# Sliding-window attention and a SoLU feed-forward layer on one core: lower weight halves by TensorE, a new order at the start, and a lag of one tile

## The chip, the core and the metric

The kernel runs on one core of one Trainium2 chip. A core has five engines that run their own instruction queues in order and meet at semaphores: TensorE (PE; its weight loads are PEld), VectorE (DVE), ScalarE (ACT), GpSimd (POOL) and SyncE (SP), which here only issues DMAs. The metric is the device time of one execution in microseconds (us). The median of three runs of the kernel before is 604.31 us (603.89 to 605.40).

## The reference

Eight batches of 576 tokens, eight heads of 64 columns, give 4608 rows of 512 columns. Attention looks back over a window of 64 tokens, and its output goes through a feed-forward layer with an inner width of 1024:

```python
scores = scale * np.matmul(q, k.transpose(0, 1, 3, 2))
mask = (rel >= 0) & (rel < window)
...
attn = np.exp(scores)
attn = attn / (np.sum(attn, axis=-1, keepdims=True) + 1e-09)
x = np.matmul(attn, v)            # regrouped to 4608 x 512
h = x @ w_in                      # 512 -> 1024
sm = np.exp(h - h_max) / (sum + 1e-09)
solu = h * sm
ln = (solu - mu) / np.sqrt(var + 1e-06) * g_ln
return ln @ w_out                 # 1024 -> 512
```

q, k, v are float32. w_in and w_out come as 64-bit floats.

## The kernel before

**Tiles.** The 4608 rows are 36 tiles of 128 rows. For each tile t the kernel runs:

- `load(t)`: DMAs of q, k and v.
- `scores(t)`: 32 small matmuls into the PSUM tile pS.
- `softmax(t)`: on DVE eight mask-and-minimum operations (L353), on ACT eight exponentials (L358), on DVE the sums' reciprocals (L366, L369), on POOL eight scalings (L371).
- `transposes(t)`: on PE (L387) in two groups of four into the PSUM tile t, copied by ACT and by DVE to PT (L392).
- `values(t)`: 32 matmuls into pX (L411), copied by ACT as the upper half xH (L417) and by DVE as the lower half xL (L418).
- `moe_in(t, h)`: 12 matmuls for each half h of the 1024 columns, into pH (L434).
- `moe_norm(t)`: DVE maximum (L449), ACT exponential (L451), DVE product and sum (L454), ACT squares (L460), a few 128x1 steps, a power on POOL (L467), and on POOL the scaled result e in two halves (L471).
- `moe_transpose(t)`: PE (L491), ACT cast to yH (L495), DVE yL (L497).
- `moe_out(t)`: 24 matmuls into pO (L508), a copy (L515) and the output's DMA (L516).

Products of the feed-forward layer are made as upper x upper, upper x lower and lower x upper, with the halves in a faster float32 form of TensorE (fp32r). pS, pH, pX and pO have one buffer each, so `moe_in(t+1, 0)` waits until `moe_norm(t)` has read pH for the last time, in L454.

**Weights.** `weight_block` turns one 128x512 block of a 64-bit weight into its two halves: a DMA of the raw words (L255), ACT's absolute value of the upper word (L256), DVE's clamp (L257), three integer steps on DVE (L259, L261, L263), for w_out a multiplication by g on POOL (L266), ACT's cast to the upper half (L268), and POOL's subtraction that gives the lower half (L269). Blocks 0 to 7 are w_in (0 to 3 the first half of the columns), 8 to 15 are w_out. The raw words have 4 buffers, the work tile wt has 3. This runs once, at the start.

**Order.** The body only records operations in a `Plan`: engine, estimated cost, tiles read and written. `Plan.edges` turns tiles, buffer rings and program order into dependencies; operations on PE also keep the program's order among each other, and the first uses of a ring's tiles begin in the program's order. `Plan.order` gives each operation a due time, walked back from PE's sequence, and then, engine by engine, takes the ready operation that is due first. The outcome is each engine's fixed queue; the costs have no other effect. The main loop puts `moe_in`, `moe_norm` and the attention of later tiles in iteration t, and `moe_transpose` and `moe_out` of tile t - BEHIND, with BEHIND = 3. So `moe_in` of tiles 0 to 3 runs before the first `moe_out`.

Of the kernel before, what the change touches and what calls it, by code (L numbers as in the profile page):

```python
# [9 lines left out]
F32 = mybir.dt.float32  # L10
# [13 lines left out]
NEG = -8.0e9  # L24

AHEAD = 3
BEHIND = 3

URGENT = 300

# [9 lines left out]
class Plan:  # L40
# [8 lines left out]
        self.tiles = {}  # L49
        self.ops = []  # L50

    def op(self, engine, cost, emit, reads, writes, lat=0):
        self.ops.append((engine, cost, emit, reads, writes, lat + self.LATENCY))

    def dma(self, size, emit, reads, writes):
        self.op("SP", max(350, size // 250), emit, reads, writes, 2000)

    def edges(self):

        before = [dict() for _ in self.ops]  # L60
        writer, readers, users, pe = {}, {}, {}, None
        for i, (engine, _, _, reads, writes, _) in enumerate(self.ops):
            for key in reads + writes:
                if key in writer:
                    before[i][writer[key]] = True
            for key in writes:
                for j in readers.pop(key, ()):
                    before[i][j] = True
                writer[key] = i
            for key in reads:  # L70
                readers.setdefault(key, []).append(i)
            for key in reads + writes:
                if key[0] in self.rings:
                    users.setdefault(key[:2], []).append(i)
            if engine == "PE":
                if pe is not None:
                    before[i].setdefault(pe, False)
                pe = i
        for (tag, n), at in users.items():
            instances = [m for g, m in users if g == tag]  # L80
            place = instances.index(n)
            if place >= self.rings[tag]:
                for j in users[tag, instances[place - self.rings[tag]]]:
                    for i in at:
                        if j != i:
                            before[i][j] = True
            if place:

                j = users[tag, instances[place - 1]][0]
                if j != at[0]:  # L90
                    before[at[0]].setdefault(j, False)
        for i, b in enumerate(before):
            b.pop(i, None)
        return before

    def order(self):
# [16 lines left out]
        for i, o in enumerate(self.ops):  # L113
            if o[0] == "PE":
                due[i] = clock
                clock += o[1]
        for j in reversed(topo):
            for i, whole in after[j]:
                lat = self.ops[j][5] if self.ops[i][0] != self.ops[j][0] else 0
                due[j] = min(due[j], due[i] - (self.ops[j][1] + lat if whole else 0))  # L120
        left = [len(b) for b in before]
        ready = [0] * n
        free = dict.fromkeys(("PE", "DVE", "ACT", "POOL", "SP"), 0)
# [27 lines left out]
def tile_window_attention_solu_moe(  # L151
# [80 lines left out]
    def weight_block(i, src, wH, wL, g, key):  # L234


        n = wH.shape[-1]

        def raw():
            return T("raw", i, [P, n, 2], I32)  # L240

        def t():
            return T("wt", i, [P, n], I32)

        def tf():
            return t().bitcast(F32)

        def lo():
            return raw()[:, :, 0]

        def hi():
            return raw()[:, :, 1]

        R, W = ("raw", i), ("wt", i)
        plan.dma(P * n * 8, lambda: nc.sync.dma_start(raw().rearrange("p n w -> p (n w)"), src), [], [R])  # L255
        plan.op("ACT", 600, lambda: nc.scalar.activation(tf(), hi().bitcast(F32), AF.Abs), [R], [W])  # L256
        plan.op("DVE", 420, lambda: nc.vector.tensor_scalar(  # L257
            tf(), tf(), EXP_LO, EXP_HI, ALU.max, ALU.min), [W], [W])
        plan.op("DVE", 420, lambda: nc.vector.tensor_scalar(  # L259
            t(), t(), 0x07FFFFFF, 3, ALU.bitwise_and, ALU.logical_shift_left), [W], [W])  # L260
        plan.op("DVE", 680, lambda: nc.vector.scalar_tensor_tensor(  # L261
            t(), hi(), -0x40000000, t(), ALU.bitwise_and, ALU.bitwise_or), [R, W], [W])
        plan.op("DVE", 680, lambda: nc.vector.scalar_tensor_tensor(  # L263
            t(), lo(), 29, t(), ALU.logical_shift_right, ALU.bitwise_or), [R, W], [W])
        if g is not None:
            plan.op("POOL", 700, lambda: nc.gpsimd.tensor_scalar(  # L266
                tf(), tf(), g, 0.0, ALU.mult, ALU.add), [W, ("g",)], [W])
        plan.op("ACT", 600, lambda: nc.scalar.copy(wH, tf()), [W], [("H", *key)])  # L268
        plan.op("POOL", 1300, lambda: nc.gpsimd.tensor_sub(wL, tf(), wH.bitcast(F32)),  # L269
                [W, ("H", *key)], [("L", *key)])  # L270

    def prep(i):
        if i < 2 * NC:
# [19 lines left out]
    def V(t, half):  # L293
        return T(f"v{half}", t, [P, DM])

    def load(t):
        first = first_of(t)
        o = t * P

        plan.dma(P * P * 16, lambda: nc.sync.dma_start(  # L300
            Q(t), qT[:, :, o:o + P].rearrange("p d s -> d p s")), [], [("q", t)])
        lack = 0 if t else WIN
        plan.dma(P * P * 24, lambda: nc.sync.dma_start(
            K(t)[:, :, lack:], kT[:, :, o - WIN + lack:o + P].rearrange("p d s -> d p s")),
            [], [("k", t)])
# [19 lines left out]
    def scores(t):  # L325
# [15 lines left out]
                            PS(t)[half * WIN:(half + 1) * WIN, r, p],  # L341
                            q[rs, p, half * WIN:(half + 1) * WIN], keys, start=True, stop=True)

        plan.op("PE", 1000, emit, [("q", t), ("k", t)], [("pS", t)])

    def softmax(t):
        def cols(tag, h):
# [15 lines left out]
        def rec():  # L363
            return T("rec", t, [P, H], pool=st)
# [2 lines left out]
            rec(), T("sm", t, [P, H], pool=st), 1e-9),  # L367
            [("sm", t, h) for h in range(H)], [("rec", t)])
        plan.op("DVE", 130, lambda: nc.vector.reciprocal(rec(), rec()), [], [("rec", t)])  # L369
        for h in range(H):  # L370
            plan.op("POOL", 360, lambda h=h: nc.gpsimd.tensor_scalar(  # L371
                SS(t)[:, h], SS(t)[:, h], rec()[:, h:h + 1], 0.0, ALU.mult, ALU.add),
                [("rec", t)], [("sS", t, h)])

# [3 lines left out]
    def transposes(t):  # L378
        for x in range(2):
# [6 lines left out]
                for i in range(4):  # L386
                    nc.tensor.transpose(pA()[:, i], SS(t)[:, 4 * x + i], ident)  # L387

            plan.op("PE", 430, emit, [("sS", t, 4 * x + i) for i in range(4)], [("t", n)])
            plan.op(  # L390
                "DVE" if x else "ACT", 600, lambda x=x, pA=pA:
                (nc.vector.tensor_copy if x else nc.scalar.copy)(PT(t)[:, 4 * x:4 * x + 4], pA()),  # L392
# [11 lines left out]
    def values(t):  # L404
        def emit():
            for p in range(NPAIR):
# [6 lines left out]
                            PT(t)[:, h, ks], start=True, stop=True)  # L413

        plan.op("PE", 1100, emit, [("PT", t, x) for x in range(2)]
                + [(f"v{half}", t, x) for half in range(2) for x in range(2)], [("pX", t)])
        plan.op("ACT", 560, lambda: nc.scalar.copy(XH(t), PX(t)), [("pX", t)], [("xH", t)])  # L417
        plan.op("DVE", 620, lambda: nc.vector.tensor_sub(XL(t), PX(t), XH(t).bitcast(F32)),  # L418
                [("pX", t), ("xH", t)], [("xL", t)])
# [3 lines left out]
    def PH(t):  # L423
        return T("pH", t, [P, DFF], pool=ps_h)
# [3 lines left out]

    def moe_in(t, h):
        hs = slice(h * 512, (h + 1) * 512)  # L430
        for c in range(NC):
            for k, (x, w, keys) in enumerate((
                    (XH, w_inH, ["xH", "H"]), (XH, w_inL, ["xH", "L"]), (XL, w_inH, ["xL", "H"]))):
                plan.op("PE", 233, lambda c=c, k=k, x=x, w=w: nc.tensor.matmul(  # L434
                    PH(t)[:, hs], x(t)[:, c], w[:, c, hs],
                    start=(c == k == 0), stop=(c == NC - 1 and k == 2)),
                    [(keys[0], t), (keys[1], "in", c, h)], [("pH", t)])

    def moe_norm(t):
        def col(x):  # L440
# [79 lines left out]
            f(t, *args)  # L520


    load(0)
    for i in range(4):
        prep(i)
    scores(0)
    softmax(0)
    load(1)
    for i in range(4, 8):
        prep(i)  # L530
# [1 line left out]
    scores(1)  # L532
    softmax(1)
    values(0)
    load(2)
    scores(2)
    softmax(2)
    plan.dma(P * NF * 4, lambda: nc.sync.dma_start(g_sb, gT), [], [("g",)])
    for i in range(8, 16):
        prep(i)  # L540
    load(3)
    for t in range(NTILE + BEHIND):
        on(load, t + AHEAD + 1)
        on(moe_in, t, 0)
        on(transposes, t + 1)
        on(moe_in, t, 1)
        on(moe_norm, t)
        on(moe_transpose, t - BEHIND)
        on(values, t + 1)
        on(scores, t + AHEAD)  # L550
        on(softmax, t + AHEAD)
        on(moe_out, t - BEHIND)
# [39 lines left out]
```

## Time and profile before

| what | us |
|---|---|
| median of the runs | 604.31 |
| profiled execution, whole | 604.69 |
| its span, first to last instruction | 602.5 |
| PE busy | 563.9 |
| DVE busy | 322.0 |
| ACT busy | 313.3 |
| POOL busy | 210.2 |

The profiled execution lies 0.38 us above the median, and 2.19 us of it are outside the span. The 50.73 MB read from memory contain 8.4 MB of raw weights. A profile line of a group names the kernel line, the engine, the operation, output <- input with shapes, the count, then busy time and mean ns, then the idle time of the engine just ahead of these instructions and what ended it. A line of the timeline begins with the start and the duration in us. A line of the windows gives the window, its length, and the busy time of PE, PEld, DVE, ACT and POOL with the number of instructions, then the granted clock of TensorE, the DMA share and GB/s.

### The profile page before, as it was taken

What the parts mean: (1) busy time and instruction counts of PE and PEld (TensorE: products, weight loads), DVE (VectorE), ACT (ScalarE), POOL (GpSimd) and SP (SyncE); (2) the same over time, 40 slices, a digit from 0 to 9 for tenths busy, and PEclk for the clock granted to TensorE, in tenths of its full rate; (3) what the DMA queues carried; (4) which work ended last, traced back from release to release, by engine and by line L of the source; (5) the groups of instructions that cost most, each with busy time, mean ns of one, the idle gap of its engine ahead of it and who ended that gap; (6) DMA issues with size and microseconds to landing.
All of it is one profiled execution on the core that took longest, in us unless ns stands there. A gap on an engine that the chain in (4) does not pass through costs nothing.

```text
span 602.5 us, 12551 instructions
## 1 busy us (share of the span) xinstructions
PE 563.9 (94%) x4608; PEld 459.3 (76%) x4608; DVE 322.0 (53%) x1180; ACT 313.3 (52%) x933; POOL 210.2 (35%) x438
## 2 busy tenths in 40 slices
PE   1387699999999999999999999999999999999997
PEld 1256578888888888888888888888888888888775
DVE  6768997555555555555555555555555555554430
ACT  3467666555555555555555555555555555553421
POOL 4554668333333333333333333333333333331110
PEclk9988889999999999999999999999999999999999
DMA  8882753333333333333333333333333331000000
GB/s 296 254 262 93 204 157 95 92 91 97 93 95 98 95 97 97 94 93 96 89 98 97 96 97 97 97 97 97 97 97 97 97 97 54 18 18 18 18 36 35
DMA packets 56204, 60.97 MB, mean 101 GB/s; under 512 B 3408, under 2 KB 40272, under 8 KB 56144
## 3 DMA queue, kind: packets, MB, share of 16 engines
q1 hardware_dynamic: 56144, 60.18, 32.7%
q8 instruction: 36, 0.59, 0.4%
q14 instruction: 24, 0.20, 0.1%
HBM read 50.73 MB, written 9.44 MB: 100 GB/s over the span
## 4 chain that ended last, share of the span: by engine, by line
PE 90%; DVE 5%; ACT 2%; POOL 1%; DMA 1%; issue 1%; SPq 0%; ACTq 0%
PE pO L508 35%; PE pH L434 34%; PE pX L411 6%; PE t L387 6%; PE pS L340 5%; PE t L491 5%; DVE wt L261 1%; DMA raw<-w_in 1%; DVE wt L263 1%; DVE sS L353 1%; DVE e L454 1%; POOL sS L371 1%; ACT sS L358 1%; POOL w_inL L269 0%; DVE wt L259 0%
## 5 line engine op out<-in xcount | busy, mean ns | idle before, releaser
L371 POOL TENSOR_SCALAR sS<-sS,rec 128x128 f32<-128x128 f32 x288 | 105.0, 386 | 258.6 <-PE pO L508 257.1
L358 ACT ACTIVATE sS<-sS,nmx 128x128 f32<-128x128 f32 x288 | 112.3, 391 | 52.9 <-DVE nmx L353 52.9
L434 PE MATMUL pH<-w_inH,xH 128*128 128x512 f32 x288 | 119.2, 414 | 8.6 <-DVE mst L454 8.6
L508 PE MATMUL pO<-w_outH,yH 128*128 128x512 f32 x288 | 117.7, 409 | 1.2 <-ACT yH L495 1.2
L434 PE MATMUL pH<-w_inH,xL 128*128 128x512 f32 x288 | 116.3, 404 | 0.0
L434 PE MATMUL pH<-w_inL,xH 128*128 128x512 f32 x288 | 116.0, 403 | 0.0
L508 PE MATMUL pO<-w_outH,yL 128*128 128x512 f32 x288 | 114.3, 397 | 0.0
L508 PE MATMUL pO<-w_outL,yH 128*128 128x512 f32 x288 | 113.9, 395 | 0.0
L495 ACT CAST yH<-t 128x512 fp32r<-128x512 f32 x72 | 38.7, 589 | 101.6 <-PE t L491 101.6
L449 DVE TENSOR_REDUCE mst<-pH 128x1 f32<-128x1024 f32 x36 | 44.1, 1224 | 70.5 <-PE pH L434 70.5
L392 DVE COPY PT<-t 128x512 f32<-128x512 f32 x36 | 24.9, 691 | 89.5 <-PE t L387 89.5
L434 PEld LDWEIGHTS pH<-w_inH,xH 128*128 128x128 f32 x288 | 55.3, 192 | 21.0 <-DVE mst L454 5.8
L471 POOL TENSOR_SCALAR e<-e,mst 128x512 f32<-128x512 f32 x72 | 54.9, 769 | 41.3 <-DVE mst L468 39.9
L508 PEld LDWEIGHTS pO<-w_outH,yH 128*128 128x128 f32 x288 | 54.1, 188 | 18.5 <-ACT e L451 4.8
L434 PEld LDWEIGHTS pH<-w_inH,xL 128*128 128x128 f32 x288 | 55.4, 192 | 13.5 <-DVE xL L418 0.2
L508 PEld LDWEIGHTS pO<-w_outH,yL 128*128 128x128 f32 x288 | 54.1, 188 | 14.6 <-DVE yL L497 1.7
L434 PEld LDWEIGHTS pH<-w_inL,xH 128*128 128x128 f32 x288 | 55.5, 193 | 11.7
L508 PEld LDWEIGHTS pO<-w_outL,yH 128*128 128x128 f32 x288 | 54.2, 188 | 11.6 <-POOL w_outL L269 0.2
L392 ACT COPY PT<-t 128x512 f32<-128x512 f32 x36 | 21.1, 585 | 76.5 <-PE t L387 76.5
L353 DVE CUSTOM_DVE_ANT_0 sS<-pS,maskNone 128x128 f32<-128x128 f32 x224 | 51.3, 286 | 14.0 <-PE pS L340 14.0
L387 PE MATMUL t<-ident,sS 128*128 128x128 f32 x288 | 42.0, 283 | 12.9 <-POOL sS L371 12.7
L358 ACT ACTIVATION_READ_ACCUMULATOR sS<-sS,nmx 128x1 f32 x288 | 53.9, 187 | 0.0
(54 smaller groups left out, 722.1 us busy)
## 6 DMA issues: line engine op xcount, KB each, us to landing
v<-vS SPq DMA_DIRECT2D x64, 256.0 KB, 4.1
k<-kT SPq DMA_DIRECT2D x35, 384.0 KB, 4.0
q<-qT SPq DMA_DIRECT2D x36, 256.0 KB, 4.6
y<-ot SPq DMA_DIRECT2D x36, 256.0 KB, 2.0
raw<-w_in SPq DMA_DIRECT2D x8, 512.0 KB, 5.2
raw<-w_out SPq DMA_DIRECT2D x8, 512.0 KB, 5.2
v<-vS SPq DMA_DIRECT2D x16, 128.0 KB, 4.5
k<-kT SPq DMA_DIRECT2D x1, 256.0 KB, 7.8
```

The lines of the kernel that those rows point to most:

```text
L340: nc.tensor.matmul(PS(t)[half * WIN:(half + 1) * WIN, r, p], q[rs, p, half * WIN:(half + 1) * WIN], keys, start=True, stop=True)
L353: plan.op("DVE", 215, lambda h=h: nc.vector.tensor_tensor_reduce(SS(t)[:, h], PS(t)[:, h % 2, h // 2], mk, scale=-SCALE, scalar=BIG, op0=A ...
L358: plan.op("ACT", 390, lambda h=h: nc.scalar.activation(SS(t)[:, h], SS(t)[:, h], AF.Exp, bias=cols("nmx", h), scale=-1.0, accum_out=cols(" ...
L371: plan.op("POOL", 360, lambda h=h: nc.gpsimd.tensor_scalar(SS(t)[:, h], SS(t)[:, h], rec()[:, h:h + 1], 0.0, ALU.mult, ALU.add), [("rec", ...
L387: nc.tensor.transpose(pA()[:, i], SS(t)[:, 4 * x + i], ident)
L392: (nc.vector.tensor_copy if x else nc.scalar.copy)(PT(t)[:, 4 * x:4 * x + 4], pA()),
L411: nc.tensor.matmul(PX(t)[r * D:(r + 1) * D, p, ks], V(t, half)[:, h * D:(h + 1) * D], PT(t)[:, h, ks], start=True, stop=True)
L434: plan.op("PE", 233, lambda c=c, k=k, x=x, w=w: nc.tensor.matmul(PH(t)[:, hs], x(t)[:, c], w[:, c, hs], start=(c == k == 0), stop=(c == NC ...
L449: plan.op("DVE", 1150, lambda: nc.vector.tensor_reduce(nmax(), PH(t), axis=AX.X, op=ALU.max, negate=True), [("pH", t)], [key(0)])
L471: plan.op("POOL", 770, lambda h=h, hs=hs: nc.gpsimd.tensor_scalar(E(t)[:, hs], E(t)[:, hs], nmean(), kk(), ALU.add, ALU.mult), [key(4), ke ...
L495: plan.op("ACT", 560, lambda hs=hs, pT=pT: nc.scalar.copy(YH(t)[:, hs], pT()), [("t", n)], [("yH", t, h)])
L508: plan.op("PE", 233, lambda f=f, k=k, y=y, w=w: nc.tensor.matmul(PO(), y(t)[:, f], w[:, f], start=(f == k == 0), stop=(f == NF - 1 and k = ...
```

## The change

- Lower halves. For blocks 0 to 7 (`LOWER`) two matmuls into a PSUM tile of the ring t, identity x w (float32) and minus identity x upper half (fp32r), and an ACT copy out. For blocks 8 to 15 a DVE subtraction. POOL makes none.
- The clamp L257 goes to POOL except in blocks 0 and 1 (`QUICK`).
- The scalings of tile 0's softmax go from POOL to DVE.
- PE operations marked loose (the lower halves; `scores`, `transposes`, `values` of tiles 0 to 2) lose their fixed place in PE's order and are placed by due time. SP's DMAs now keep the program's order.
- Program order: q and k of tile 0 first, block 0, scores and softmax of tile 0, block 1, v of tile 0, blocks 2 and 3; `load(2)` between blocks 11 and 12; scores and softmax of tile 2 inside the first iteration.
- `moe_in(0, h)` sorts its passes so that those with lower weight halves come last.
- BEHIND = 1: tile t - 1 instead of t - 3 is transposed and multiplied by w_out in iteration t. The ring e falls from 4 buffers to 2.
- Estimated costs of weight steps and DMAs are changed (340 for 420, 610 for 680, 340 bytes per ns for 250).

```diff
-BEHIND = 3
+HASTE = 1
+QUICK = (0, 1)
+LOWER = range(8)
+LOOSE = 3
+BEHIND = 1
...
-            if engine == "PE":
-                if pe is not None:
-                    before[i].setdefault(pe, False)
-                pe = i
+            if engine in last and not loose:
+                if last[engine] is not None:
+                    before[i].setdefault(last[engine], False)
+                last[engine] = i
...
-                clock += o[1]
+                clock += 0 if o[6] else o[1]
...
+    minus = const.tile([P, P], F32R, name="minus")
+    nc.vector.tensor_scalar_mul(minus, ident, -1.0)
...
-        plan.op("DVE", 420, lambda: nc.vector.tensor_scalar(
+        engine, e, cost = ("DVE", nc.vector, 340) if i in QUICK else ("POOL", nc.gpsimd, 750)
+        plan.op(engine, cost, lambda: e.tensor_scalar(
             tf(), tf(), EXP_LO, EXP_HI, ALU.max, ALU.min), [W], [W])
...
-        plan.op("POOL", 1300, lambda: nc.gpsimd.tensor_sub(wL, tf(), wH.bitcast(F32)),
-                [W, ("H", *key)], [("L", *key)])
+        if i not in LOWER:
+            plan.op("DVE", 610, lambda: nc.vector.tensor_sub(wL, tf(), wH.bitcast(F32)),
+                    [W, ("H", *key)], [("L", *key)])
+            return
+        def pL():
+            return T("t", f"w{i}", [P, n], pool=ps_t)
+        def emit():
+            nc.tensor.matmul(pL(), ident, tf(), start=True, stop=False)
+            nc.tensor.matmul(pL(), minus, wH, start=False, stop=True)
+        plan.op("PE", 1150, emit, [W, ("H", *key)], [("t", f"w{i}")], loose=True)
+        plan.op("ACT", 560, lambda: nc.scalar.copy(wL, pL()), [("t", f"w{i}")], [("L", *key)])
...
+        engine, v, cost = ("POOL", nc.gpsimd, 360) if t else ("DVE", nc.vector, 150)
         for h in range(H):
-            plan.op("POOL", 360, lambda h=h: nc.gpsimd.tensor_scalar(
+            plan.op(engine, cost, lambda h=h: v.tensor_scalar(
...
+        passes = [(c, *k) for c in range(NC) for k in (
+            (XH, w_inH, "xH", "H"), (XH, w_inL, "xH", "L"), (XL, w_inH, "xL", "H"))]
+        if t == 0:
+            passes.sort(key=lambda k: k[4] == "L")
...
-    load(0)
-    for i in range(4):
-        prep(i)
+    load(0, range(2))
+    prep(0)
     scores(0)
     softmax(0)
+    prep(1)
+    load(0, range(2, 4))
+    for i in range(2, 4):
+        prep(i)
     load(1)
     for i in range(4, 8):
         prep(i)
...
     values(0)
-    load(2)
-    scores(2)
-    softmax(2)
     plan.dma(P * NF * 4, lambda: nc.sync.dma_start(g_sb, gT), [], [("g",)])
-    for i in range(8, 16):
+    for i in range(8, 12):
+        prep(i)
+    load(2)
+    for i in range(12, 16):
         prep(i)
     load(3)
     for t in range(NTILE + BEHIND):
         on(load, t + AHEAD + 1)
         on(moe_in, t, 0)
+        if t == 0:
+            scores(2)
+            softmax(2)
+        if t < BEHIND:
+            on(moe_in, t, 1)
+            on(moe_norm, t)
+            on(transposes, t + 1)
+            on(scores, t + AHEAD)
+            on(softmax, t + AHEAD)
+            on(values, t + 1)
+        else:
             on(transposes, t + 1)
             on(moe_in, t, 1)
             on(moe_norm, t)
             on(moe_transpose, t - BEHIND)
             on(values, t + 1)
             on(scores, t + AHEAD)
             on(softmax, t + AHEAD)
             on(moe_out, t - BEHIND)
```

More of the change, by code (lines that the diff above doesn't have):

```diff
@@ L50, in __init__, with op @@
         self.ops = []
-    def op(self, engine, cost, emit, reads, writes, lat=0):
-        self.ops.append((engine, cost, emit, reads, writes, lat + self.LATENCY))
+    def op(self, engine, cost, emit, reads, writes, lat=0, loose=False):
+        self.ops.append((engine, cost, emit, reads, writes, lat + self.LATENCY, loose))
     def dma(self, size, emit, reads, writes):
-        self.op("SP", max(350, size // 250), emit, reads, writes, 2000)
+        self.op("SP", max(350, size // 340), emit, reads, writes, 2000)
     def edges(self):
         before = [dict() for _ in self.ops]
-        writer, readers, users, pe = {}, {}, {}, None
-        for i, (engine, _, _, reads, writes, _) in enumerate(self.ops):
+        writer, readers, users, last = {}, {}, {}, {"PE": None, "SP": None}
+        for i, (engine, _, _, reads, writes, _, loose) in enumerate(self.ops):
             for key in reads + writes:
@@ L119, in order @@
                 lat = self.ops[j][5] if self.ops[i][0] != self.ops[j][0] else 0
-                due[j] = min(due[j], due[i] - (self.ops[j][1] + lat if whole else 0))
+                due[j] = min(due[j], due[i] - (HASTE * (self.ops[j][1] + lat) if whole else 0))
         left = [len(b) for b in before]
@@ L256, in weight_block @@
         plan.op("ACT", 600, lambda: nc.scalar.activation(tf(), hi().bitcast(F32), AF.Abs), [R], [W])
-        plan.op("DVE", 420, lambda: nc.vector.tensor_scalar(
+        engine, e, cost = ("DVE", nc.vector, 340) if i in QUICK else ("POOL", nc.gpsimd, 750)
+        plan.op(engine, cost, lambda: e.tensor_scalar(
             tf(), tf(), EXP_LO, EXP_HI, ALU.max, ALU.min), [W], [W])
-        plan.op("DVE", 420, lambda: nc.vector.tensor_scalar(
+        plan.op("DVE", 340, lambda: nc.vector.tensor_scalar(
             t(), t(), 0x07FFFFFF, 3, ALU.bitwise_and, ALU.logical_shift_left), [W], [W])
-        plan.op("DVE", 680, lambda: nc.vector.scalar_tensor_tensor(
+        plan.op("DVE", 610, lambda: nc.vector.scalar_tensor_tensor(
             t(), hi(), -0x40000000, t(), ALU.bitwise_and, ALU.bitwise_or), [R, W], [W])
-        plan.op("DVE", 680, lambda: nc.vector.scalar_tensor_tensor(
+        plan.op("DVE", 610, lambda: nc.vector.scalar_tensor_tensor(
             t(), lo(), 29, t(), ALU.logical_shift_right, ALU.bitwise_or), [R, W], [W])
@@ L294, in V, with load @@
         return T(f"v{half}", t, [P, DM])
-    def load(t):
+    def load(t, parts=range(4)):
         first = first_of(t)
         o = t * P
-        plan.dma(P * P * 16, lambda: nc.sync.dma_start(
-            Q(t), qT[:, :, o:o + P].rearrange("p d s -> d p s")), [], [("q", t)])
         lack = 0 if t else WIN
-        plan.dma(P * P * 24, lambda: nc.sync.dma_start(
-            K(t)[:, :, lack:], kT[:, :, o - WIN + lack:o + P].rearrange("p d s -> d p s")),
-            [], [("k", t)])
+        if 0 in parts:
+            plan.dma(P * P * 16, lambda: nc.sync.dma_start(
+                Q(t), qT[:, :, o:o + P].rearrange("p d s -> d p s")), [], [("q", t)])
+        if 1 in parts:
+            plan.dma(P * P * 24, lambda: nc.sync.dma_start(
+                K(t)[:, :, lack:], kT[:, :, o - WIN + lack:o + P].rearrange("p d s -> d p s")),
+                [], [("k", t)])
         for half in range(2):
             i = o + (half - 1) * WIN
+            if 2 + half not in parts:
+                continue
             if first == half:
@@ L342, in emit @@
                             q[rs, p, half * WIN:(half + 1) * WIN], keys, start=True, stop=True)
-        plan.op("PE", 1000, emit, [("q", t), ("k", t)], [("pS", t)])
+        plan.op("PE", 1000, emit, [("q", t), ("k", t)], [("pS", t)], loose=t < LOOSE)
     def softmax(t):
@@ L387, in emit @@
                     nc.tensor.transpose(pA()[:, i], SS(t)[:, 4 * x + i], ident)
-            plan.op("PE", 430, emit, [("sS", t, 4 * x + i) for i in range(4)], [("t", n)])
+            plan.op("PE", 430, emit, [("sS", t, 4 * x + i) for i in range(4)], [("t", n)], loose=t < LOOSE)
             plan.op(
@@ L415, in values @@
         plan.op("PE", 1100, emit, [("PT", t, x) for x in range(2)]
-                + [(f"v{half}", t, x) for half in range(2) for x in range(2)], [("pX", t)])
+                + [(f"v{half}", t, x) for half in range(2) for x in range(2)], [("pX", t)],
+            loose=t < LOOSE)
         plan.op("ACT", 560, lambda: nc.scalar.copy(XH(t), PX(t)), [("pX", t)], [("xH", t)])
@@ L430, in moe_in @@
         hs = slice(h * 512, (h + 1) * 512)
[L431 to L437, printed above, removed]
+        passes = [(c, *k) for c in range(NC) for k in (
+            (XH, w_inH, "xH", "H"), (XH, w_inL, "xH", "L"), (XL, w_inH, "xL", "H"))]
+        if t == 0:
+            passes.sort(key=lambda k: k[4] == "L")
+        for n, (c, x, w, xk, wk) in enumerate(passes):
+            plan.op("PE", 233, lambda n=n, c=c, x=x, w=w: nc.tensor.matmul(
+                PH(t)[:, hs], x(t)[:, c], w[:, c, hs],
+                start=(n == 0), stop=(n == len(passes) - 1)),
+                [(xk, t), (wk, "in", c, h)], [("pH", t)])
     def moe_norm(t):
@@ L534, in tile_window_attention_solu_moe @@
     values(0)
+    plan.dma(P * NF * 4, lambda: nc.sync.dma_start(g_sb, gT), [], [("g",)])
+    for i in range(8, 12):
+        prep(i)
     load(2)
-    scores(2)
-    softmax(2)
-    plan.dma(P * NF * 4, lambda: nc.sync.dma_start(g_sb, gT), [], [("g",)])
-    for i in range(8, 16):
+    for i in range(12, 16):
         prep(i)
@@ L544, in tile_window_attention_solu_moe @@
         on(moe_in, t, 0)
[L545 to L552, printed above, removed]
+        if t == 0:
[9 more added lines that the diff above has]
+        else:
+            on(transposes, t + 1)
+            on(moe_in, t, 1)
+            on(moe_norm, t)
+            on(moe_transpose, t - BEHIND)
+            on(values, t + 1)
+            on(scores, t + AHEAD)
+            on(softmax, t + AHEAD)
+            on(moe_out, t - BEHIND)
     order = plan.order()
```

## The prediction

> **What bounds the kernel now.** I read the page first, then the windows of its stages, then the chain of waits, then the groups of the slow stage.
>
> ```profile
> span 602.5 us, 12551 instructions
> PE 563.9 (94%) x4608; PEld 459.3 (76%) x4608; DVE 322.0 (53%) x1180; ACT 313.3 (52%) x933; POOL 210.2 (35%) x438
> ...
> 0.00:33.00 33.00, 9.50 (x137) 6.77 (x138) 24.18 (x64) 15.56 (x42) 15.39 (x32) 1.00 0.84 265
> ...
> 0.00:88.30 88.30, 54.53 (x532) 41.59 (x533) 69.96 (x198) 51.17 (x151) 48.24 (x83) 0.92 0.67 211
> ...
> 93.20:569.50 476.30, 476.30 (x3930) 392.86 (x3929) 238.87 (x952) 252.11 (x764) 155.00 (x345) 1.00 0.28 85
> 569.50:602.50 33.00, 28.14 (x129) 20.99 (x127) 8.43 (x17) 8.71 (x16) 2.07 (x3) 1.00 0.09 33
> ```
>
> From 93.2 to 569.5 PE never pauses: there the time is PE's work, and the change alters none of it. What can move is the start, where PE is busy 9.50 of the first 33 us and DVE 69.96 of 88.3, and the tail. The chain gives the price of each PE step at full clock:
>
> ```profile
> 40.20 4.28 PE pH L434 x12
> ...
> 93.21 2.80 PE pH L434 x12
> 96.02 0.87 PE t L387 x8
> ...
> 99.70 0.87 PE t L491 x8
> 100.58 1.08 PE pX L411 x32
> 101.66 1.03 PE pS L340 x32
> 102.69 5.79 PE pO L508 x24
> ```
>
> A half of `moe_in` takes 2.80 us (4.28 on a throttled clock), `transposes` 0.87, `moe_transpose` 0.87, `values` 1.08, `scores` 1.03, `moe_out` 5.79.
>
> **How an edit at the start becomes time.** Take the end of the first `moe_out` as the mark; before, it is at 93.2. By then PE has done 8 halves of `moe_in`, 5 `transposes`, 5 `values`, 7 `scores`, one `moe_transpose`, one `moe_out`: 22.4 + 4.35 + 5.4 + 7.2 + 0.87 + 5.79 = 46.0 us. With a lag of one, at the same mark, it has done 4 halves, 3 `transposes`, 3 `values`, 5 `scores`, and the last two: 11.2 + 2.6 + 3.2 + 5.15 + 6.66 = 28.9. It still owes 17.1 us more, so if T is the new mark and PE runs without pause behind it, the gain at the start is 93.2 - 17.1 - T = **76.1 - T**. The shorter lag by itself saves no PE work. It removes the waits of PE for the one buffer pH, which arise because the first `moe_in` have no `moe_out` between them:
>
> ```profile
> PE pH L434 <- DVE mst L454: 8.6, 3, 3.4
> ```
>
> Those 8.6 us go, but w_out is then needed two tiles earlier, and what is late next is its preparation on DVE.
>
> **DVE's ledger up to the mark.** Its groups in the window from 0 to 88.3, which ends with block 15's last integer step:
>
> ```profile
> L261 DVE SCALAR_TENSOR_TENSOR wt<-raw,wt 128x512 int32<-128x512 int32 x16 | 15.4, 962 | 0.3
> L263 DVE SCALAR_TENSOR_TENSOR wt<-raw,wt 128x512 int32<-128x512 int32 x16 | 12.8, 803 | 0.2
> L257 DVE TENSOR_SCALAR wt<-wt 128x512 f32<-128x512 f32 x16 | 9.4, 590 | 7.7 <-ACT wt L256 7.7
> L259 DVE TENSOR_SCALAR wt<-wt 128x512 int32<-128x512 int32 x16 | 7.5, 466 | 0.3
> ...
> L449 DVE TENSOR_REDUCE mst<-pH 128x1 f32<-128x1024 f32 x4 | 4.9, 1219 | 3.1 <-PE pH L434 3.1
> L454 DVE CUSTOM_DVE_ANT_0 e<-pH,e 128x1024 f32<-128x1024 f32 x3 | 3.7, 1218 | 0.0
> ...
> L392 DVE COPY PT<-t 128x512 f32<-128x512 f32 x5 | 3.4, 689 | 5.1 <-PE t L387 5.1
> L418 DVE TENSOR_TENSOR xL<-pX,xH 128x512 fp32r<-128x512 f32 x4 | 2.7, 684 | 0.5 <-ACT xH L417 0.5
> ...
> 4.71 0.43 DVE L257 TENSOR_SCALAR wt<-wt 128x512 f32<-128x512 f32 x1 [4.71 <-ACT wt L256]
> ...
> 20.71 0.69 DVE L263 SCALAR_TENSOR_TENSOR wt<-raw,wt 128x512 int32<-128x512 int32 x1
> ...
> 30.18 0.20 DVE sS L353
> ```
>
> Undisturbed, L257 and L259 take 0.43 and L261 and L263 0.69; the groups' sums are 9.3 us above 16 times these (4.4 + 1.8 + 2.5 + 0.6). The excess comes from POOL:
>
> ```profile
> 14.64 1.26 POOL L269 TENSOR_TENSOR w_inL<-wt,w_inH 128x512 fp32r<-128x512 f32 x1 [2.00 <-ACT w_inH L268]
> ...
> 14.75 1.71 DVE L261 SCALAR_TENSOR_TENSOR wt<-raw,wt 128x512 int32<-128x512 int32 x1
> ...
> 56.93 0.69 POOL L266 TENSOR_SCALAR wt<-wt,g_sb 128x512 f32<-128x512 f32 x1
> ...
> 65.16 1.07 POOL L266 TENSOR_SCALAR wt<-wt,g_sb 128x512 f32<-128x512 f32 x1 [3.25 <-DVE wt L263]
> ...
> 65.90 0.61 DVE L257 TENSOR_SCALAR wt<-wt 128x512 f32<-128x512 f32 x1
> ```
>
> While POOL subtracts (L269), DVE's L261 stands 1.0 us; beside a POOL operation with one input (L266, undisturbed 0.69) DVE's L257 loses 0.18, and POOL's takes 1.07. The ledger, from 69.96 us:
>
> 1. Work of later tiles, no longer due: two softmaxes, 16 x 0.20 = 3.2; two PT copies 1.4; one xL 0.7; of four maxima and three L454 I keep one and a half each, since tile 1's norm falls half ahead of the mark: 3.05 + 1.8. Together -10.1.
> 2. Fourteen clamps to POOL: 14 x 0.43 = -6.0.
> 3. Excess: L269 is gone, 14 clamps and 8 multiplications by g remain as one-input POOL operations: 22 x 0.18 = 4.0 in place of 9.3: -5.3.
> 4. Eight lower halves on DVE, nearest row L418: 8 x 0.68 = +5.4.
> 5. Tile 0's eight scalings of 128x128, between a quarter of L257's 0.43 and the whole of it (0.9 to 3.4): 0.2 each, nearest the 128x128 step L353, +1.6.
>
> That is 55.5 us. **Idle time:** DVE stands 88.3 - 70.0 = 18.3 us before, 4.7 of it until its first instruction. That start moves later, because q and k (0.5 MB) go ahead of the first raw block:
>
> ```profile
> 3.00:25.00 22.00, 2.93 (x34) 1.98 (x34) 18.54 (x42) 9.71 (x27) 9.55 (x14) 1.00 0.99 317
> ...
> 36.94 20.16 SPq L255 DMA_DIRECT2D raw<-w_out  x4
> ```
>
> At 317 GB/s that is 1.6 us: 6.3. The other 13.6 are in the groups: 3.0 for ACT's first step (7.7 less 4.7), whose tile wt waited for L269 of three blocks earlier; 5.1 for `transposes`; 3.1 for `moe_in`; some 2.4 in small pieces. The first goes with L269. Of the next two I take half, since PE still runs one queue on which tile 1 waits for tile 0. The rest stays: 4.1 + 2.4 = 6.5. Behind DVE's last subtraction three matmuls remain, 0.7. So **T = 6.3 + 55.5 + 6.5 + 0.7 = 69.0**, and the start gains 7.1 us.
>
> **What I cost at nothing, and its cover.** The lower halves by PE are one fp32r matmul of 128x512 (2.80 / 12 = 0.23) and one float32: at least four 128-column steps of the transposes (4 x 0.11 = 0.44), at most four throttled matmuls (4 x 0.36). Eight pairs take 5.4 to 14.3 us, inside the 23.5 us in which PE stands idle ahead of 33 us. Without that cover each us counts. ACT gets eight copies of about 0.6; it was busy 51 of 88 us. SP's fixed order adds a wait: `load(3)` stands behind raw block 15, which waits for block 11's buffer, and `scores(3)` stands ahead of `moe_in(1, 0)` on PE. DVE reaches the end of block 11 at about 47 us by the same prices (12 blocks 21.7, clamps 0.9, four halves 2.7, three softmaxes with reciprocals 6.3, scalings 1.6, PT and xL 1.4, excess and idle 6, start 6.3), q and k land near 51, and from there 2 x 2.80 + 0.87 + 0.87 + 1.08 + 2 x 1.03 + 5.79 = 16.3 leads to 67.3, below 69.0. It is covered by 1.7 us. The fixed order replaces the stretch above in which four w_out DMAs hang in SP's queue for 20.16 us.
>
> **The tail.**
>
> ```profile
> 569.46 1.04 PE L491 MATMUL t<-ident,e 128*128 128x128 f32 x8
> ...
> 576.60 1.52 POOL L471 TENSOR_SCALAR e<-e,mst 128x512 f32<-128x512 f32 x2 [0.40 <-DVE mst L468]
> 576.78 1.03 PE L491 MATMUL t<-ident,e 128*128 128x128 f32 x8
> ...
> 578.11 0.50 PE L508 MATMUL pO<-w_outH,yH 128*128 128x512 f32 x1 [0.29 <-ACT yH L495]
> ```
>
> `moe_transpose` to `moe_out` without cover takes 1.33 instead of 0.87, four times before, twice with the short lag: 0.9 saved. But then tile 35 is transposed at once behind tile 34's `moe_out`, at the place of 576.78, and its e is half ready at 576.60 + 0.76 = 577.36: 0.6 lost. Net gain 0.3.
>
> Sum: 7.1 + 0.3 = 7.4 us; the profiled 604.69 becomes 597.3, and since it lies 0.38 above the median, the forecast is 604.31 - 7.4 = **596.9**.
>
> **A rule weighed against the rows.** The row is the pair at 65.16 and 65.90: DVE loses 0.18, POOL 0.38. The Trainium skill, "SBUF — State Buffer", section "SBUF: two separate sides", says that the ports shared by DVE and GpSimd are an exclusive lock, held by whichever starts first for its whole instruction. The L269 pair agrees (1.71 beside 1.26); the L266 pair shows DVE mostly the winner. By the rule clamps on POOL could cost DVE their full length; that is the third rival.
>
> **The rivals.**
>
> - *DVE never waits.* If due times now bring every operand in time, the idle term is 0: T = 62.5, gain 13.6 + 0.3, **590.4**. For it: three of DVE's waits have causes that the change touches. Against it: the wait on SP above would bind at about the same time, and PE starts on a throttled clock.
> - *The idle time stays.* All 13.6 us remain: T = 76.1, gain 0 + 0.3, **604.0**. For it: DVE's waits for PE come from tile 0's chain, which stays serial; `transposes(0)` now also stands behind block 7's lower half in the ring t.
> - *The clamps hold DVE's port.* Each of the 22 POOL operations stops DVE for the length of one, 0.69: 15.2 in place of 4.0, T = 80.2, **608.1**, slower. It decides against the change from T = 76.4, that is from (76.4 - 69.0) / 22 + 0.18 = 0.5 us per operation. Against it: the 0.18 of the row.
> - *The norm becomes a wait of every tile.* In the steady stage it uses nearly a whole period:
>
> ```profile
> 341.96 1.52 POOL L471 TENSOR_SCALAR e<-e,mst 128x512 f32<-128x512 f32 x2 [1.34 <-DVE mst L468]
> ...
> 343.59 1.03 PE L491 MATMUL t<-ident,e 128*128 128x128 f32 x8
> ```
>
> A period is 2 x 2.80 + 0.87 + 0.87 + 1.08 + 1.03 + 5.79 = 15.24, so `moe_in` ended at 328.35 and e is complete at 343.48. With a lag of three nobody needs it; with one it is needed at 343.59. From 0.6 us more (the second half is read 0.5 later) each tile waits: 0.3 us over cost 35 x 0.3 = 10.5, about 608. Against it: due times now put the norm ahead of softmax, and at the end, without competition, it takes 577.36 - 569.46 = 7.9.
>
> **How the numbers follow.** The forecast's case has 0.55, no waiting 0.22, the idle kept 0.10, the port 0.08, the norm 0.05. A difference under 0.3% (1.8 us) can't be told from no change. Faster 0.55 + 0.22 = 0.77, same 0.10, slower 0.13. The range reaches from below 590.4 by the 2 us that the scalings and PE's pairs leave open to the kept idle: 588.5 to 604.5.
>
> **What would show it.** Right: the mark near 69; PE without pause behind it; no PE wait for L454; L261 and L263 below 0.8 in the mean; DVE idle 10 to 15 us up to the mark; the tail within 0.5 us of now. Wrong: PE pauses before L491 in the middle (norm); L261 above 1.0 (port); DVE idle above 18 us; PE waiting for q or k of tile 3 longest; a mark set by ACT.

## The result

The changed kernel takes 609.18 us (median of four runs, 609.01 to 609.37) against 604.31: a ratio of 1.0078, 95% interval 1.0066 to 1.009. It is slower by 4.9 us, where 596.9 was forecast. Its profiled execution takes 609.37, with a span of 607.6, 5.1 above the span before.

The page and the windows of the changed kernel up to the mark (the end of the first `moe_out`), from there to the last `moe_in`, and the tail:

```profile
span 607.6 us, 12692 instructions
PE 575.6 (95%) x4632; PEld 463.4 (76%) x4632; DVE 317.5 (52%) x1183; ACT 321.9 (53%) x941; POOL 216.3 (36%) x428
...
0.00:81.50 81.50, 54.09 (x384) 34.87 (x385) 57.39 (x158) 44.70 (x119) 50.91 (x59) 0.85 0.60 189
...
81.50:582.90 501.40, 501.40 (x4162) 413.78 (x4161) 254.15 (x1013) 270.81 (x811) 162.00 (x365) 1.00 0.29 89
582.90:607.60 24.70, 20.10 (x89) 14.73 (x87) 5.95 (x13) 6.36 (x11) 3.37 (x5) 0.97 0.09 33
```

Behind the mark PE never pauses up to 582.9, so a shorter lag costs the steady stage nothing. All of the loss stands ahead of the mark. The mark is read where the last of the 24 matmuls gives way to the next matmul on PE, at 81.5 (their records overlap):

```profile
81.28 0.39 PE L542 MATMUL pO<-w_outH,yL 128*128 128x512 f32 x1
81.50 0.40 PE L468 MATMUL pH<-w_inH,xH 128*128 128x512 f32 x1
```

By the prediction's rule the start then loses 81.5 - 76.1 = 5.4 us, the tail gives 0.3 back, and the span should grow by 5.1: it did, from 602.5 to 607.6. Both parts of the rule also hold by themselves. PE's busy time behind the mark is 501.40 + 20.10 = 521.50 us, against 476.30 + 28.14 = 504.44 before, so 17.06 are owed; PE's idle time in the tail is 24.70 - 20.10 = 4.60 against 33.00 - 28.14 = 4.86. So the rule was right and T was wrong. DVE is busy for 57.39 us up to there; the ledger said 55.5. Most of what exceeds the forecast is idle time: 81.5 - 57.4 = 24.1 us instead of 6.3 + 6.5 + 0.7 = 13.5. The groups of DVE and of POOL in that window show where (line numbers are those of the changed kernel: L269 is now the clamp, L271, L273 and L275 are the integer steps, L278 the multiplication by g, L282 DVE's subtraction for the lower half):

```profile
L273 DVE SCALAR_TENSOR_TENSOR wt<-raw,wt 128x512 int32<-128x512 int32 x16 | 12.8, 799 | 0.4
L275 DVE SCALAR_TENSOR_TENSOR wt<-raw,wt 128x512 int32<-128x512 int32 x16 | 11.9, 742 | 0.4
L271 DVE TENSOR_SCALAR wt<-wt 128x512 int32<-128x512 int32 x16 | 7.8, 485 | 12.2 <-POOL wt L269 11.9
...
L282 DVE TENSOR_TENSOR w_outL<-wt,w_outH 128x512 fp32r<-128x512 f32 x8 | 5.3, 695 | 1.6 <-ACT w_outH L280 1.6
```

```profile
L269 POOL TENSOR_SCALAR wt<-wt 128x512 f32<-128x512 f32 x14 | 28.4, 2033 | 22.5 <-ACT wt L266 12.3 <-PE t_w L292 10.1
L401 POOL TENSOR_SCALAR sS<-sS,rec 128x128 f32<-128x128 f32 x16 | 8.8, 565 | 0.0
L278 POOL TENSOR_SCALAR wt<-wt,g_sb 128x512 f32<-128x512 f32 x8 | 7.1, 891 | 3.2 <-DVE wt L275 3.2
```

A clamp takes 2.03 us on POOL, a multiplication by g on the same tile 0.89. DVE did the clamp in 0.43. The integer steps stand close to their undisturbed times (0.80, 0.74 and 0.49 against 0.69, 0.69 and 0.43, together 3.5 us over 16 blocks), so POOL slows little of what DVE executes; DVE stands in front of the first integer step, L271, and waits for the clamp. One such wait in the timeline:

```profile
30.81 1.92 POOL L269 TENSOR_SCALAR wt<-wt 128x512 f32<-128x512 f32 x1 [2.12 <-ACT wt L266]
...
32.77 0.43 DVE L271 TENSOR_SCALAR wt<-wt 128x512 int32<-128x512 int32 x1 [1.86 <-POOL wt L269]
```

Late weights then hold SP's fixed order: the DMAs of four w_out blocks take 14.00 us of its queue, since each waits for a raw buffer that DVE's last integer step frees. q and k of tile 3 stand behind them and come late, and PE waits 4.00 us:

```profile
37.62 14.00 SPq L265 DMA_DIRECT2D raw<-w_out  x4
...
58.25 1.98 PE L369 MATMUL pS<-k,q 64*64 64x128 f32 x32 [4.00 <-DMA k<-kT]
```

### The profile page after: what moved, and what is told of

Its sections match the earlier page's. It is cut to its first block, busy times and chain, and to the rows that moved or that the text cites. A ratio compares the mean times of both kernels' runs of the same rounds, so it can differ in the third digit from the quotient of the medians.

```text
span 607.6 us, 12692 instructions
## 1 busy us (share of the span) xinstructions
PE 575.6 (95%) x4632; PEld 463.4 (76%) x4632; DVE 317.5 (52%) x1183; ACT 321.9 (53%) x941; POOL 216.3 (36%) x428
## 4 chain that ended last, share of the span: by engine, by line
PE 86%; POOL 5%; DVE 3%; DMA 2%; issue 2%; ACT 1%; SPq 0%; POOLq 0%; ACTq 0%
PE pO L542 33%; PE pH L468 31%; PE pX L441 6%; PE pS L369 6%; PE t L525 5%; PE t L417 5%; POOL wt L269 3%; DMA raw<-w_in 1%; DMA k<-kT 1%; POOL sS L401 1%; POOL wt L278 1%; POOL e L505 1%; DVE wt L275 1%; DVE wt L273 0%; DVE e L488 0%
## 5 line engine op out<-in xcount | busy, mean ns | idle before, releaser
L501 POOL TENSOR_TENSOR mst<-mst,neghalf 128x1 f32<-128x1 f32 x36 | 19.8, 551 | 317.2 <-DVE mst L499 317.2
L468 PE MATMUL pH<-w_inH,xH 128*128 128x512 f32 x288 | 117.3, 407 | 0.0
L468 PE MATMUL pH<-w_inH,xL 128*128 128x512 f32 x288 | 114.5, 397 | 0.1
L468 PE MATMUL pH<-w_inL,xH 128*128 128x512 f32 x288 | 113.4, 397 | 0.0
L401 POOL TENSOR_SCALAR sS<-sS,rec 128x128 f32<-128x128 f32 x280 | 101.6, 388 | 22.5 <-DVE rec L398 18.5
L494 ACT ACTIVATE sq<-e,mst 128x1024 bf16<-128x1024 f32 x36 | 41.5, 1151 | 47.4 <-DVE mst L492 45.8
```

The source lines that it names most:

```text
L401: plan.op(engine, cost, lambda h=h: v.tensor_scalar(SS(t)[:, h], SS(t)[:, h], rec()[:, h:h + 1], 0.0, ALU.mult, ALU.add), [("rec", t)], [( ...
L468: plan.op("PE", 233, lambda n=n, c=c, x=x, w=w: nc.tensor.matmul(PH(t)[:, hs], x(t)[:, c], w[:, c, hs], start=(n == 0), stop=(n == len(pas ...
L494: plan.op("ACT", 1200, lambda: nc.scalar.activation(T("sq", t, [P, DFF], BF16), E(t), AF.Square, bias=nmean(), scale=1.0, accum_out=ss()), ...
```

## The experiments

Theory C: the clamp's duration on POOL is the cause. Rivals: SP's order (S), the port shared by DVE and POOL (P), the shorter lag itself (L). All ratios are against the kernel before in the same session, with 95% intervals. The medians of the kernel before lie between 603.78 and 604.64 in these sessions, so times of different sessions can differ by some 0.9 us without a cause in the kernel. An edit marked "all clamps on DVE" is made on the changed kernel with QUICK = range(16).

### Only the operation of POOL's clamp

```diff
-        plan.op(engine, cost, lambda: e.tensor_scalar(
-            tf(), tf(), EXP_LO, EXP_HI, ALU.max, ALU.min), [W], [W])
+        lims = (EXP_LO, EXP_HI, ALU.max, ALU.min) if i in QUICK else (1.0, 0.0, ALU.mult, ALU.add)
+        plan.op(engine, cost, lambda: e.tensor_scalar(tf(), tf(), *lims), [W], [W])
```

> The changed kernel with POOL's 14 clamps replaced by a multiplication by 1 and an addition of 0 on the same tile, so the limits on the exponents are left out in blocks 2 to 15. Theory C in the form that it is the operations max and min that are slow on POOL: the POOL step takes 0.7 to 1.1 us instead of 1.9, DVE's wait of 11.9 us goes, the mark falls to 69 to 72 and the time to 597 to 600. Rival P (any POOL step at this place collides with DVE for the port): it stays near 1.9 us, and the time near 609.

598.35 us, ratio 0.9902 (0.9887 to 0.9917). This is the cleanest test: the estimated cost is unchanged, so every engine's queue holds the same instructions in the same order as in the changed kernel (the two traces agree in this on all five engines). POOL's step, DVE's wait for it, the window up to the mark and the mark, in this order:

```profile
L270 POOL TENSOR_SCALAR wt<-wt 128x512 f32<-128x512 f32 x14 | 10.6, 757 | 28.3 <-ACT wt L266 28.3
...
L271 DVE TENSOR_SCALAR wt<-wt 128x512 int32<-128x512 int32 x16 | 7.8, 489 | 3.2 <-POOL wt L270 3.2
...
0.00:70.40 70.40, 49.38 (x385) 32.31 (x386) 57.23 (x158) 45.08 (x119) 32.17 (x59) 0.90 0.69 219
...
70.15 0.40 PE L542 MATMUL pO<-w_outH,yL 128*128 128x512 f32 x1
```

The step takes 0.76 instead of 2.03, DVE's wait for it falls from 11.9 to 3.2, and the mark from 81.5 to 70.4. Of the 11.1 us, 8.7 are that wait; nearly all the rest is other idle time of DVE. P falls: a POOL step in the same place, on the same tile, beside the same DVE work hardly stops DVE (its L273 takes 0.78 in the mean there, 0.80 in the changed kernel).

### All clamps back on DVE

```diff
-QUICK = (0, 1)
+QUICK = range(16)
```

> The changed kernel with all 16 clamps on DVE again. The mark is the end of the first moe_out, 81.5 us in the changed kernel. Theory C (the clamp takes 1.9 us on POOL and DVE waits for it): DVE's 11.9 us of waiting for POOL's clamp go, 14 x 0.43 = 6.0 us of DVE work come back, the mark falls to about 75.5 and the time to about 603. Rival S (SP's fixed order with the short lag: q and k of tile 3 land late, and scores(3) holds PE): the mark stays within 1 us of 81.5 or rises by the 6 us of DVE work, 609 to 615.

599.61 us, ratio 0.9922 (0.9908 to 0.9937), 3.4 us better than C said. Two of DVE's groups, the window up to the mark, and PE's wait for q and k of tile 3:

```profile
L275 DVE SCALAR_TENSOR_TENSOR wt<-raw,wt 128x512 int32<-128x512 int32 x16 | 11.3, 712 | 0.4
L273 DVE SCALAR_TENSOR_TENSOR wt<-raw,wt 128x512 int32<-128x512 int32 x16 | 11.3, 705 | 0.4
...
0.00:71.50 71.50, 48.54 (x385) 32.76 (x386) 61.17 (x176) 44.20 (x119) 19.68 (x46) 0.94 0.68 216
...
51.04 1.10 PE L369 MATMUL pS<-k,q 64*64 64x128 f32 x32 [1.35 <-DMA k<-kT]
```

The mark is 71.5, where C said 75.5. Half of the difference is DVE's work, which grows by 3.8 us and not by 6.0: without POOL's clamps beside them the steps L273 and L275 are 2.1 us shorter. The other half is idle time, which falls from 24.1 to 10.3: I had removed only the waits named for POOL, 11.9 us, and not those behind them. PE's wait for k of tile 3, for one, shrinks from 4.00 to 1.35 us. S falls as the main cause, since SP's order is the same here.

### Which operation is slow

In short (blocks 0 and 1 keep the clamp on DVE):

```diff
+        if 2 <= i < 6:    max with EXP_LO, add 0        # L273 in this kernel
+        elif 6 <= i < 11: min with EXP_HI, add 0        # L276
+        elif i >= 11:     max with EXP_LO alone         # L279
```

> The changed kernel with POOL's clamp split for its duration: blocks 2 to 5 take the maximum and add 0, blocks 6 to 10 the minimum and add 0, blocks 11 to 15 the maximum alone in one operation. If each of max and min costs its share: 1.2 to 1.4 us in the first two groups. If a single max or min already puts POOL on the slow way: 1.9 in all three. If only the pair is slow: 0.7 in all three. The limits left out change the result only for weights beyond them.

606.32 us, from a single execution. One step of each kind, from POOL's timeline:

```profile
21.41 1.92 POOL L273 TENSOR_SCALAR wt<-wt 128x512 f32<-128x512 f32 x1 [4.01 <-ACT wt L266]
...
29.91 1.92 POOL L276 TENSOR_SCALAR wt<-wt 128x512 f32<-128x512 f32 x1 [2.12 <-ACT wt L266]
...
55.08 1.49 POOL L279 TENSOR_SCALAR wt<-wt 128x512 f32<-128x512 f32 x1 [4.38 <-ACT wt L266]
```

A max or a min paired with an addition takes the same 1.92 us as max with min. A max alone takes 1.49 in three of its five steps and 1.92 in the other two. One of them is enough; a multiplication with an addition takes 0.69. What POOL does differently inside, and why two of the single steps are longer, is not shown here.

### The lag, in three surroundings

```diff
-BEHIND = 3     # the kernel before
+BEHIND = 1
```

> The kernel before with a lag of one tile as its only edit. By the prediction's ledger DVE loses 10 us of later tiles' work ahead of the mark of 93.2, so the mark comes to about 80 to 83 against a break-even of 76.1: 607 to 611, slower. If instead the lag by itself gives its 8.6 us of waits for pH back: about 596.

605.89 us, ratio 1.0021 (1.001 to 1.0032): slower, but by 1.4 and not by 3 to 7. The first of 24 matmuls starts early, at 66.21, and the fifteenth waits for tile 0's lower half yL behind weight steps on DVE; the last one and the next matmul on PE give the mark:

```profile
72.69 0.80 PE L508 MATMUL pO<-w_outH,yL 128*128 128x512 f32 x1 [2.96 <-DVE yL L497]
...
76.70 0.63 PE L508 MATMUL pO<-w_outH,yL 128*128 128x512 f32 x1
77.13 0.63 PE L434 MATMUL pH<-w_inH,xH 128*128 128x512 f32 x1
```

The mark is 77.1, near the break-even of 76.1; the ledger had 80 to 83.

```diff
-BEHIND = 1     # the changed kernel
+BEHIND = 3
```

> The changed kernel with a lag of three tiles as before. Theory C: the first two halves of moe_in still end at about 53.1, 8.7 us later than in the kernel before (44.4), since POOL's clamps hold back w_in too, and the waits for the one buffer pH return: 610 to 615. Rival L (the shorter lag is what costs): 604 or below.

613.77 us, ratio 1.0164 (1.0147 to 1.0181), as C said. PE waits for pH again:

```profile
PE pH L468 <- DVE mst L488: 4.3, 3, 1.9
```

The short lag is not what costs; in the changed kernel it is worth 613.77 - 609.18 = 4.6 us.

```diff
-QUICK = (0, 1)
+QUICK = range(16)
-BEHIND = 1     # the changed kernel
+BEHIND = 3
```

> The changed kernel with all clamps on DVE and the lag of three tiles of the kernel before. It prices the shorter lag in a kernel without the slow clamps (599.6 with a lag of one). If the lag is worth what the mark says there: with a lag of three the waits for the one buffer pH return, so 605 to 609. If w_out's preparation eats the gain of the shorter lag, as it did in the kernel before with a lag of one (605.9 against 604.5): 598 to 600.

605.25 us, ratio 1.0017 (1.0005 to 1.0028). Here too PE waits for pH:

```profile
PE pH L468 <- DVE mst L488: 3.5, 2, 1.9
```

So with all clamps on DVE the short lag is worth 605.25 - 599.61 = 5.6 us, and in the kernel before it is worth nothing. Without the short lag the other parts of the change are worth nothing either (605.25). Only the two together gain. Slow weights alone don't explain why the lag fails in the kernel before: the changed kernel has the later mark, and gains 4.6 us by it. Which part of the change lets the lag pay is not shown.

### The lower halves

```diff
-LOWER = range(8)     # all clamps on DVE
+LOWER = ()
-            plan.op("DVE", 610, lambda: nc.vector.tensor_sub(wL, tf(), wH.bitcast(F32)),
+            plan.op("POOL", 1300, lambda: nc.gpsimd.tensor_sub(wL, tf(), wH.bitcast(F32)),
```

> The changed kernel with all clamps on DVE and all 16 lower halves by POOL's subtraction, as in the kernel before. If POOL's two-input step is what stopped DVE there (1.0 us each, 9.3 in all) and its removal is what the change is worth, the mark rises by 9.3 less the 8 subtractions of 0.68 that DVE no longer makes, about 4 us: 603 to 605. If the lower halves on PE, ACT and DVE are worth nothing: 599 to 600.

609.04 us, ratio 1.0072 (1.0052 to 1.0092): 9.4 us worse than with the lower halves on PE, ACT and DVE, twice what was expected. DVE's four weight steps up to that kernel's mark:

```profile
L273 DVE SCALAR_TENSOR_TENSOR wt<-raw,wt 128x512 int32<-128x512 int32 x16 | 18.1, 1136 | 0.4
L275 DVE SCALAR_TENSOR_TENSOR wt<-raw,wt 128x512 int32<-128x512 int32 x16 | 12.5, 787 | 0.4
...
L271 DVE TENSOR_SCALAR wt<-wt 128x512 int32<-128x512 int32 x16 | 10.0, 630 | 0.4
L269 DVE TENSOR_SCALAR wt<-wt 128x512 f32<-128x512 f32 x16 | 8.9, 557 | 1.5 <-ACT wt L266 1.5
```

Together they stand 13.9 us above 16 times their undisturbed times (9.3 in the kernel before, 1.3 in clamps_dve), and DVE is busy for 70.55 us up to the mark at 81.6, 9.4 more than in clamps_dve. This is where POOL stops DVE: by its two-input step. Its one-input steps hardly do.

```diff
-LOWER = range(8)     # all clamps on DVE
+LOWER = range(12)
```

> The changed kernel with all clamps on DVE and the lower halves of blocks 8 to 11 by PE and ACT too. If DVE's work sets the mark, four subtractions of 0.68 go: 2.7 us less, about 597. If PE, which takes 1.0 to 2.0 us for each pair, or ACT takes DVE's place: 599.5 to 602.

598.35 us, ratio 0.9897 (0.988 to 0.9914), 1.3 us better than with eight, half of the 2.7 us that DVE was relieved of.

```diff
-LOWER = range(8)     # all clamps on DVE
+LOWER = range(16)
```

> The changed kernel with all clamps on DVE and all 16 lower halves by PE and ACT. If DVE still sets the mark at 12 blocks (598.35), the last four subtractions bring another 1 to 2 us: 596.5 to 598. If PE, which now makes four pairs more while moe_in and moe_out wait behind them, takes its place: 598.5 to 602.

606.39 us, ratio 1.0043 (1.0031 to 1.0054), far worse than either case. The pairs of w_out now stand in PE's queue ahead of tile 0's `moe_in` and between its matmuls, and wait there for POOL's multiplication by g, 3.4 us in three waits. One of them:

```profile
43.62 1.67 PE L291 MATMUL t_w<-wt,ident 128*128 128x512 f32 x2 [1.67 <-POOL wt L278]
```

That this order costs the rest of the 8 us was read from the trace and not tested by itself.

### The start and SP's order

```diff
-    load(0, range(2))     # all clamps on DVE
     prep(0)
+    load(0, range(2))
```

> The changed kernel with all clamps on DVE and the first raw block's DMA ahead of q and k of tile 0, as it nearly was in the kernel before. DVE's first weight step begins at 9.7 us in the changed kernel and at 4.7 before; the prediction had 6.3. If the start sets the mark: 2 to 4 us less than 599.6, 596 to 598. If softmax of tile 0, which then begins later, fills the same place on DVE: 599 to 600.5.

599.1 us, ratio 0.9926 (0.9907 to 0.9946): no difference from 599.61 that these runs can tell. DVE's first weight step begins at 4.57 instead of 9.38, and the mark comes at 71.1 instead of 71.5: with the later start, softmax of tile 0 fills DVE's time ahead of the weights.

```diff
-"PE": None, "SP": None     # all clamps on DVE
+"PE": None
```

> The changed kernel with all clamps on DVE and SP's DMAs placed by due time as in the kernel before, instead of in the program's order. If the fixed order helps by bringing w_out's raw blocks and q and k in the needed order: 601 to 606. If it costs, because q and k of tile 3 stand behind raw block 15: 596 to 599.

599.93 us, ratio 0.9931 (0.9905 to 0.9957), runs from 597.29 to 601.87. Also no difference that shows; with the clamps on DVE, SP's fixed order costs nothing. In the changed kernel itself it was not tested.

```diff
+QUICK = range(16), LOWER = range(12), load(0, range(2)) behind prep(0)
```

> The two edits together on the changed kernel with all clamps on DVE: lower halves of blocks 8 to 11 by PE and ACT too, and the first raw block ahead of q and k. If the mark with 12 blocks is still set by DVE's chain from its first step on, the earlier start shows now: 596 to 598. If it is set by PE's queue or by later waits, as the two single edits suggest (1.3 and 0.5 us, the second within the spread): 598 to 599.

603.41 us, ratio 0.9987 (0.9976 to 0.9997): one edit that gained 1.3 us and one without an effect that shows lose 5.1 us together against the first alone. In the chain of waits POOL's scalings of one softmax stand ahead of the norm's steps, whose L501 begins at 57.78 in lower12:

```profile
59.16 5.29 POOL sS L401 x8
64.44 0.54 POOL mst L501
65.00 0.65 DVE mst L502
```

Each edit that touches a cost, an engine or the program's order is planned anew, and the queues around the mark come out differently. That this placement costs the 5 us was read from the chain and not tested by itself.

### The mark as a measure

The prediction's rule gives the span as 602.5 - (76.1 - T) - 0.3. With T from the first matmul behind the first `moe_out`, for every kernel with a lag of one:

| kernel | T | span by the rule | span |
|---|---|---|---|
| changed | 81.5 | 607.6 | 607.6 |
| pool_mult | 70.4 | 596.5 | 596.5 |
| clamps_dve | 71.5 | 597.6 | 598.1 |
| pool_split | 78.5 | 604.6 | 604.5 |
| before_lag1 | 77.1 | 603.2 | 603.9 |
| lower_pool | 81.6 | 607.7 | 607.6 |
| lower12 | 70.8 | 596.9 | 596.8 |
| lower16 | 78.5 | 604.6 | 604.9 |
| raw_first | 71.1 | 597.2 | 597.2 |
| sp_free | 72.7 | 598.8 | 598.7 |
| lower12_raw_first | 75.8 | 601.9 | 601.9 |

The two largest misses, 0.5 and 0.7 us, have a cause behind the mark. In clamps_dve and before_lag1 the next half of `moe_in` starts while the granted clock is 0.50, and takes 3.27 and 3.44 us instead of 2.80.

## Why the prediction was wrong

**The step that failed** is the ledger's second and third item, "Fourteen clamps to POOL: 14 x 0.43 = -6.0" and the "14 clamps and 8 multiplications by g" as one-input POOL operations. They count what DVE saves and what it loses to collisions, and price a clamp on POOL as another L266, 0.69, which multiplies and adds. No row of the trace before showed a max or a min on POOL; I bounded neither its duration nor the wait of DVE for it, and the idle term holds nothing for that wait. The clamp measured 1.92 undisturbed and 2.03 in the mean, on the chain of each weight block ahead of DVE's first integer step, and DVE waited 11.9 us for it. With a POOL step that does take 0.76, the same queues gave a mark of 70.4 against a forecast of 69.0, and 598.35 us against 596.9: the rest of the sum stands, in part because errors of opposite sign cancel in it (below).

Point by point:

- *The mark and 17.1 us of PE work owed:* right; the table above.
- *PE's waits for pH go with the short lag:* right for the changed kernel, where none is left; they return in after_lag3 and clamps_dve_lag3. The lag alone does not remove them all: 2.4 of 8.6 us stay in before_lag1, and 0.6 come up in pool_mult. What is late next is w_out's preparation, as said.
- *Excess from L269 goes:* right. Its return in lower_pool cost 9.4 us, where about 4 were expected. *4.0 us from one-input steps:* 3.5.
- *DVE's work 55.5 us:* 57.39, of which 1.2 are tile 1's norm, which falls ahead of the mark as a whole and not by half.
- *Start at 6.3:* the first weight step came at 9.73, since the first raw block took 7.25 us to land behind q and k. DVE ran tile 0's first masks in that time, so 8.0 us of it were idle.
- *Idle 6.5 us behind the start:* right only without the slow clamp. In pool_mult all idle time up to the mark is 70.4 - 57.2 = 13.2, where 6.3 + 6.5 and a tail of 0.7 were forecast; 7.9 of it lie ahead of the first weight step and 5.3 behind it. The sum is better than its two parts, and that is luck.
- *Lower halves by PE, 5.4 to 14.3 us, covered:* they kept PE busy for 16.58 us, above the upper end (14.28 in pool_mult), and PE stood idle for 27.4 us up to the mark.
- *SP's fixed order covered by 1.7 us:* it held PE for 4.00 us, because block 11 left DVE at 51.2 instead of 47. In pool_mult block 11 is done at 44.2, and PE waits 0.66.
- *Tail +0.3:* right.
- *The rivals:* the third, 608.1, and the norm, about 608, came closest in time, but neither mechanism occurred. The third would have shown as L273 above 1.0 in the mean; L273 is 0.80, and DVE's loss is idle time in front of L271. The norm never became a wait: PE does not pause from 81.5 to 582.9.

The exclusive lock of the Trainium skill, "SBUF — State Buffer", section "SBUF: two separate sides", agrees with POOL's subtraction (L273 at 1.14 in lower_pool). It does not agree with POOL's one-input steps: in the changed kernel L273 began 0.05 us behind a clamp, and took 1.10 us while the clamp ran for 1.92. By the lock it would have stood until the clamp was done:

```profile
33.18 1.92 POOL L269 TENSOR_SCALAR wt<-wt 128x512 f32<-128x512 f32 x1 [0.45 <-ACT wt L266]
...
33.23 1.10 DVE L273 SCALAR_TENSOR_TENSOR wt<-raw,wt 128x512 int32<-128x512 int32 x1
```

So the third rival's condition did not hold. Another page bears on the step that failed. The Trainium skill, "GPSIMD Engine Reference", section "4.1 Engine selection", advises VectorE for elementwise add, mul and max, and adds that GpSimd runs one-input steps at roughly line rate. Beside DVE's 0.43 for the clamp, POOL's multiplication at 0.69 may pass for that; its max at 1.49 to 1.92 does not, and here the measurement decides. The page's advice to use VectorE was sound for the clamp: clamps_dve is 9.6 us faster than the changed kernel.

## What to carry to other kernels

An operation moved to another engine needs a row for that operation on that engine; a neighbour with the same shape but other arithmetic is no price, and without one the sum needs an upper end that includes the wait of the engine left behind. Where PE runs gap-free behind a start, one mark and the PE work owed there turned every edit of the start into time within a microsecond here. Where a planner lays out the queues anew for each edit, edits of one microsecond need not add up, as lower12_raw_first shows: compare kernels with the same order, as pool_mult with the changed kernel, before naming a cause.

## What the runs showed that I had not expected

- POOL's max or min on 128x512 float32 takes 1.92 us with a second operation, and a max alone 1.49 to 1.92; multiplication and addition take 0.62 to 0.69 undisturbed.
- A float32 identity matmul with its fp32r partner takes 2.28 us from one pair to the next at a granted clock of 0.50 (26.92 to 29.20) and 1.10 at full clock (46.12 to 47.22 in lower12), the first above my upper end of 1.8:

```profile
26.92 2.05 PE L291 MATMUL t_w<-wt,ident 128*128 128x512 f32 x2 [4.73 <-DVE wt L275]
...
29.20 2.05 PE L291 MATMUL t_w<-wt,ident 128*128 128x512 f32 x2
```

```profile
46.12 1.02 PE L291 MATMUL t_w<-wt,ident 128*128 128x512 f32 x2
...
47.22 1.02 PE L291 MATMUL t_w<-wt,ident 128*128 128x512 f32 x2
```

- Per step, POOL's one-input work loses more beside DVE's than the reverse. Up to the mark of pool_mult POOL's 128x128 scalings take 0.54 in the mean against 0.38 in the steady stage, and L278 0.83 against 0.69; DVE's integer steps take 0.49, 0.78 and 0.74 against 0.43, 0.69 and 0.69. Half of the scalings are not slowed at all (median 0.38).
